# A transformer layer on one core: the same operations with a new issue order, new PSUM banks and eviction engines, and another pairing of the first layer's remainders

## The chip, the core and the metric

The kernel runs on one core of a Trainium2 chip. TensorE (PE, with its weight loads shown as PEld) multiplies; VectorE (DVE), ScalarE (ACT) and GpSimd (POOL) work on elements; the queue of SyncE (SP) issues every DMA. Each engine takes its instructions strictly in the order in which they were written, and engines wait for each other through semaphores. The metric is the device time of one execution in microseconds: 462.19 us before, the median of three runs (461.88 to 462.23).

## The reference

The input x has 2048 rows of 576 (bfloat16). It is computed:

```python
h  = x + A(layernorm(x))
h2 = h + gelu(layernorm(h) @ w1 + b1) @ w2 + b2       # w1: 576 x 4608
```

A is attention with 32 heads of 18 over four segments of 512 rows, with a memory carried from segment to segment:

```python
for s in range(4):
    p = softmax(qs @ ks.T * scale + causal_mask);  a_dot = p @ vs
    a_mem = (phi(qs) @ M) / (phi(qs) @ z + 1e-6)
    outs.append(g * a_mem + (1 - g) * a_dot)
    M += phi(ks).T @ vs;  z += phi(ks).sum(rows)
return concat(outs) @ wo                              # phi(t) = t+1 if t > 0 else exp(t)
```

## The kernel before

The rows are worked in eight chunks of 256, each of two tiles of 128 rows. For each tile: a layernorm (DVE statistics at L874/L883, POOL for the root at L878/L879, DVE or ACT to apply it at L887/L895), a transpose of the result (on PE at L910 for the first tiles, by a DMA transpose at L570 later), the products with wqkv (L867/L868, five matmuls for a contraction of 576: four of 128 and one remainder), evictions of q, k and v from PSUM (L994 to L1012), and transposes of q and k into QT and KT (PE at L1032 or DMA at L570). Attention goes in 80 visits: a score group of 16 matmuls into the four banks of `st` (L1115, tiled by 32 rows), one exp on ACT (L1132), masks on POOL (L1136), and groups of weighted values into the bank `ox` (L1155, tiled by 32 columns). One set of `st` banks serves all visits, so a score group waits until the exp of the visit before has read it. L1199 to L1209 finish a head group; L1169 to L1190 are the memory's part; L1309 transposes the attention's output, L867 multiplies it with wo, L1321 adds x, and a second layernorm follows.

The first layer of the MLP multiplies by w1 in half-groups (class `Half`, L1370) of two column blocks of 128, 256 rows wide. Its contraction of 576 is four times 128 and a remainder of 64. There are two forms. `whole` does the five matmuls one after the other over the full array (L867, L868). Or the remainders of two half-groups are issued together as a `rest` of four matmuls (L1390, `tail`), which use the upper and the lower 64 rows of the array side by side, and the 16 main matmuls follow (L1396, `main`). The set `WHOLE` names the rests (by their number) that are not issued in that way but as `whole`. Bias and eviction are at L1472 (DVE) or L1470 (ACT), gelu at L1488 (ACT), the second layer at L1588 with its eviction at L1594, and the output stores at L1598/L1600. Weights of w1 come group by group through SP (L1355, with two tails at L1358), w2 once (L1364, L1726).

A planner inside the kernel (from L65 on) builds a list `ops` of some 2,590 operations; but the order in which they are issued is not the planner's. It is written out as the list `ORDER` (L1737), which holds numbers of that list, and the last lines issue them in that order under a manual schedule. Number 81 is a filler, a matmul of zeros (L1652) that PE runs while it waits at the start; it stands 29 times in the list. Three more tables change the operations themselves: `PLACE` gives the PSUM bank (0 to 2) for the n-th time that a bank is taken, where it is not the planner's own; `FLIP` lists evictions that go to the other engine of DVE and ACT (or of ACT and POOL); `WHOLE` as above. Semaphores follow from the data and the banks, so a new order or a new bank gives new waits.

```python
        if o.made in FLIP:
            o.issue = issue
...
            return dict.__getitem__(self, ("bank", PLACE.get(k.n, k[1])) if isinstance(k, Tok) else k)
...
            h.rest = o.made not in WHOLE and o
...
        for n in ORDER:
            ops[n].issue()
```

Of the kernel before, what the change touches and what calls it, by code (L numbers as in the profile page):

```python
# [16 lines left out]
def kernel(  # L17
# [118 lines left out]
    class Tok(tuple):  # L136
# [22 lines left out]
    }  # L159
    FLIP = {  # L160
# [5 lines left out]
    }  # L166
    WHOLE = {
        2534, 2535, 2536, 2537, 2539, 2542, 2544, 2548, 2550, 2551, 2552, 2565, 2567, 2575,
# [1554 lines left out]
    for j, one in sorted(bulk.items()):  # L1723
# [182 lines left out]
```

## Time and profile before

| | before |
|---|---|
| reported time, median of 3 | 462.19 us |
| span of the profiled execution | 458.6 us |
| busy PE / ACT / DVE / POOL | 451.2 / 329.6 / 272.8 / 223.1 us |
| moved by DMA | 78.39 MB, mean 171 GB/s |
| granted TensorE clock | 1.000 over the span |

The span runs from the first to the last instruction; the reported time has some 3.6 us more around it. "Busy" is the time in which an engine has an instruction under way. A matmul's duration in the trace (0.27 us for 256 columns) is longer than its distance to the next one (0.11 us), since matmuls are pipelined: for the length of PE's work the starts count, not the durations. A row of the timeline is: start, time until the last of the group ends, engine, line, operation, what it writes and reads, shapes, count, and in brackets the idle time before it with what ended that. "SPq" is the queue in which DMAs are issued.

### The profile page before, as it was taken

How to read it: one execution, taken by the hardware profiler on the slowest of the kernel's cores; microseconds unless marked ns; L12 is line 12 of the kernel's file. 1: busy time of each engine (PE TensorE's matmuls, PEld its weight loads, DVE VectorE, ACT ScalarE, POOL GpSimd, SP SyncE). 2: the span in 40 equal slices, each digit the busy share in tenths (PEclk: the TensorE clock that was granted, in tenths of full speed). 3: DMA queues.
4: the chain of work that ended last, by engine and by line, in shares of the span. 5: the costliest groups of instructions: out<-in, count | busy, mean ns of one | idle time of the engine just before them, and what ended most of it. 6: DMA issues, size and time to landing. Idle time of an engine off the chain costs nothing.

```text
span 458.6 us, 14459 instructions
## 1 busy us (share of the span) xinstructions
PE 451.2 (98%) x6102; PEld 338.9 (74%) x6102; DVE 272.8 (59%) x604; ACT 329.6 (72%) x324; POOL 223.1 (49%) x378
## 2 busy tenths in 40 slices
PE   7998999999999999999999999999999999999997
PEld 5655688676787776777677767777777778888876
DVE  6897888887765686776566587655454323321111
ACT  8887888997698977979678897787756513363610
POOL 5785667687756478874545578764151100000000
PEclk9999999999999999999999999999999999999999
DMA  8689987958887934968778577965665439773011
GB/s 223 179 150 262 263 245 184 257 127 198 162 189 157 253 87 137 186 172 197 155 131 182 161 166 168 222 202 177 158 188 161 143 97 226 223 230 92 27 53 51
DMA packets 113091, 78.39 MB, mean 171 GB/s; under 512 B 47571, under 2 KB 110979, under 8 KB 113027
## 3 DMA queue, kind: packets, MB, share of 16 engines
q1 hardware_dynamic: 113027, 77.48, 68.6%
q8 instruction: 47, 0.77, 0.7%
q14 instruction: 17, 0.14, 0.1%
HBM read 60.09 MB, written 7.08 MB: 146 GB/s over the span
## 4 chain that ended last, share of the span: by engine, by line
PE 94%; DMA 2%; DVE 2%; ACT 1%; SPq 1%; issue 1%; ACTq 0%
PE bank L1588 23%; PE bank L867 20%; PE bank L1396 16%; PE last L1588 6%; PE st L1115 6%; PE bank L868 5%; PE ox L1155 5%; PE last L1396 4%; PE bank L1390 3%; PE ox L1588 2%; PE bank L1184 1%; DMA KT<-hT 1%; PE ox L1396 1%; DMA x_b<-in_A_x_dram 1%; ACT pt L1132 1%; PE bank L1080 1%
## 5 line engine op out<-in xcount | busy, mean ns | idle before, releaser
L1132 ACT ACTIVATE pt<-st 128x2048 bf16<-128x2048 f32 x80 | 150.1, 1877 | 41.0 <-PE st L1115 37.9
L1588 PEld LDWEIGHTS <-hT 128*128 128x128 bf16 x1188 | 112.0, 98 | 26.5
L1588 PE MATMUL bank<-w_sb,hT 128*128 128x288 bf16 (+1 forms) x864 | 121.8, 284 | 0.0
L1136 POOL TENSOR_SCALAR_AFFINE_SELECT pt<-pt 128x512 bf16<-128x512 bf16 x128 | 80.1, 640 | 51.5 <-ACT pt L1132 46.8
L1472 DVE TENSOR_TENSOR hT<-bank,b1T 128x512 bf16<-128x512 f32 x96 | 65.3, 687 | 60.7 <-PE bank L1396 48.9
L1396 PEld LDWEIGHTS <-w1g 128*128 128x128 bf16 x672 | 62.4, 98 | 15.1 <-issue 7.2
L1396 PE MATMUL bank<-xn2T,w1g 128*128 128x256 bf16 x576 | 72.7, 273 | 0.0
L1488 ACT ACTIVATE hT<-hT 128x1536 bf16<-128x1536 bf16 (+4 forms) x25 | 66.2, 2661 | 4.3 <-DVE hT L1472 4.1
L867 PE MATMUL bank<-wqkv,xT 128*128 128x432 bf16 (+2 forms) x256 | 56.0, 341 | 0.9 <-DVE xT L968 0.5
L867 PEld LDWEIGHTS <-xT 128*128 128x128 bf16 x392 | 35.9, 98 | 21.5 <-DVE xT L968 0.8
L1470 ACT ACTIVATE hT<-bank,b1T 128x256 bf16<-128x256 f32 x46 | 19.3, 472 | 33.4 <-PE bank L1396 24.8
L1115 PE MATMUL st<-QT,KT 32*128 32x128 bf16 x1280 | 32.3, 217 | 1.7 <-DMA KT<-hT 1.3
L867 PE MATMUL bank<-xn2T,w1g 128*128 128x256 bf16 (+1 forms) x264 | 33.8, 260 | 0.0
L1588 PE MATMUL last<-w_sb,hT 128*128 128x288 bf16 (+1 forms) x252 | 33.4, 277 | 0.0
L1174 POOL TENSOR_TENSOR pq<-ek,pq 128x512 bf16<-128x512 bf16 x24 | 28.0, 1167 | 7.5 <-DVE ek L1172 6.7
L1115 PEld LDWEIGHTS <-KT 32*128 32x128 bf16 x1280 | 18.7, 92 | 16.9 <-issue 11.1
L1199 DVE STREAM_TRANSPOSE ox<-ox 128x512 f32<-128x512 f32 x32 | 23.3, 728 | 11.4 <-PE ox L1155 11.4
L867 PEld LDWEIGHTS <-w1g 128*128 128x128 bf16 x272 | 24.0, 98 | 3.5
L1155 PE MATMUL ox<-pt,v_aug 128*19 128x128 bf16 x1280 | 25.8, 220 | 0.0
L1321 DVE TENSOR_TENSOR h_t<-bank,x_b 128x288 f32<-128x288 f32 x32 | 14.3, 454 | 18.8 <-PE bank L868 15.5
L1155 PEld LDWEIGHTS <-v_aug 128*19 128x19 bf16 x1280 | 17.9, 91 | 9.1 <-issue 7.4
L1209 POOL TENSOR_TENSOR o_nat<-t,t 128x288 bf16<-128x288 f32 x24 | 19.1, 794 | 9.4 <-DVE t L1208 9.3
(143 smaller groups left out, 666.5 us busy)
## 6 DMA issues: line engine op xcount, KB each, us to landing
w1g<-in_B_w_dram SPq DMA_DIRECT2D x57, 512.0 KB, 4.1
w_sb<-in_B_w_dram SPq DMA_DIRECT2D x12, 432.0 KB, 4.8
wqkv<-in_B_w_dram SPq DMA_DIRECT2D x10, 512.0 KB, 5.0
hd<-h_t SPq DMA_DIRECT2D x16, 288.0 KB, 3.2
hc<-hd SPq DMA_DIRECT2D x32, 144.0 KB, 2.4
w1g<-in_B_w_dram SPq DMA_DIRECT2D x114, 32.0 KB, 3.3
x_b<-in_A_x_dram SPq DMA_DIRECT2D x18, 144.0 KB, 3.6
hT<-in_B_w_dram SPq DMA_DIRECT2D x5, 512.0 KB, 5.1
```

The costliest lines, as they stand in the source:

```text
L867: nc.tensor.matmul(out=out_ap, lhsT=lhsT_of(slice(0, P), k), rhs=rhs_of(slice(0, P), k), start=(k == 0), stop=False)
L868: nc.tensor.matmul(out=out_ap, lhsT=lhsT_of(slice(0, rest), 4), rhs=rhs_of(slice(0, rest), 4), start=False, stop=True)
L1115: nc.tensor.matmul(out=st4[:, i, n * P:(n + 1) * P], lhsT=KTs[(2 * (c - c % 2) + kt) % NK][rows, g, :], rhs=QTs[(2 * c + qt) % NQ][rows, g ...
L1132: op("ACT", 1.88, lambda: nc.scalar.activation(out=pt[:], in_=st4[:], func=ACT.Exp, scale=scale), sk, [("pt", slot, n) for n in range(4)], ...
L1136: op("POOL", 0.65, lambda n=n: nc.gpsimd.affine_select(out=pt[:, :, n * P:(n + 1) * P], in_=pt[:, :, n * P:(n + 1) * P], pattern=[[0, 4], ...
L1155: nc.tensor.matmul(out=ox[32 * i:32 * i + E, (g % 4) * P:(g % 4) * P + P], lhsT=v_augs[(2 * s0 + kt) % NV][:, G * i + g, :], rhs=pts[slot] ...
L1174: op("POOL", 1.16, lambda: nc.gpsimd.tensor_tensor(out=pq[:], in0=e_g, in1=pq[:], op=ALU.add), ["ek"], ["pq"], slack=due("add"))
L1199: op("DVE", 0.73, lambda: nc.vector.transpose(out=ox[:], in_=ox[:]), [], ["ox"], slack=slack)
L1396: nc.tensor.matmul(out=self.acc[:, a, :], lhsT=self.wt[:, k, f:f + P], rhs=xn2T[self.c % 4][:, k, :], start=False, stop=(k == 3), skip_gro ...
L1472: either((0.684, lambda: nc.vector.tensor_tensor(out=dst, in0=acc(), in1=bias, op=ALU.add)), (nj * (0.22 + w * 0.00098), by_act), [b, "b1T ...
L1488: op("ACT", (f1e - f0) * Q * 0.00083 + 0.18, lambda: nc.scalar.activation(out=hT[:, f0:f1e, :], in_=hT[:, f0:f1e, :], func=ACT.Gelu_apprx_ ...
L1588: nc.tensor.matmul(out=bank_of(b)[:, 0:w], lhsT=hT[:, q, tl * P:(tl + 1) * P], rhs=w2_sb[:, q, hs], start=(q == 0), stop=(q == NF - 1))
```

## The change

The four tables are replaced; every other line stays (below the tables the line numbers rise by one). `ORDER` holds the same 2,558 numbers before and after, and 2,479 places hold another number. `PLACE` grows from 154 to 196 entries and `FLIP` goes from 79 to 75. `WHOLE` loses six of its numbers and gains one. Cut to the beginnings of the long tables:

```diff
     PLACE = {
-        6: 1, 7: 0, 10: 2, 11: 0, 12: 1, 15: 1, 16: 0, 19: 0, 20: 2, 22: 1, 23: 0, 26: 2, 31: 2, 32: 0, 39: 0, 40: 2,
...
+        3: 2, 5: 1, 7: 2, 8: 0, 11: 1, 12: 2, 15: 2, 16: 0, 17: 2, 19: 1, 21: 1, 22: 0, 23: 2, 24: 1, 25: 1, 27: 2,
...
     }
     FLIP = {
-        137, 161, 169, 189, 191, 221, 223, 234, 236, 238, 264, 266, 346, 422, 424, 426, 433, 436, 493, 642, 665, 667,
...
+        103, 137, 163, 177, 179, 189, 191, 221, 223, 234, 238, 264, 266, 348, 399, 422, 426, 436, 665, 671, 675, 678,
...
     }
     WHOLE = {
-        2534, 2535, 2536, 2537, 2539, 2542, 2544, 2548, 2550, 2551, 2552, 2565, 2567, 2575,
+        2534, 2536, 2539, 2542, 2548, 2550, 2552, 2565, 2570,
     }
...
     ORDER = [
-        1, 24, 26, 19, 0, 21, 22, 20, 81, 2, 81, 81, 46, 81, 64, 3, 81, 81, 62, 5, 81, 65, 18, 34, 81, 81, 8, 44, 81,
-        29, 81, 66, 4, 73, 51, 81, 11, 30, 81, 49, 9, 81, 31, 67, 81, 35, 59, 32, 81, 7, 81, 36, 54, 81, 23, 10, 81,
...
+        8, 19, 62, 24, 27, 23, 81, 81, 26, 11, 51, 81, 81, 81, 56, 52, 0, 49, 20, 42, 81, 25, 44, 81, 81, 48, 29, 28,
+        21, 22, 1, 2, 81, 81, 81, 81, 81, 81, 81, 55, 30, 81, 31, 5, 81, 18, 64, 81, 34, 3, 81, 81, 81, 81, 81, 81,
...
     ]
```

In the built kernels this gives, engine by engine:

- PE: 6,102 matmuls in both. L867/L868 lose 100, L1396/L1390 gain 80 and 20. Groups in a tiled mode go from 166 to 171 (42 to 47 of them remainders), entries into one from the full array from 97 to 93.
- SP: 392 entries in both. The first loads are x_b0, x_p0, x_p1 and then wq, where they were x_p1, x_p0 and then wq. The DMA transpose of the third K tile (KT2) stands 31st among the DMAs instead of 35th, right behind a 512 KB load of w1; one slice of wo now stands behind it.
- The first xT is copied from PSUM by ACT (L969) instead of DVE (L968); the transposes of the third tile stand ahead of the k products instead of behind them.
- Evictions of the first layer on DVE (L1472) go from 110 to 106, the ACTIVATEs of L1470 on ACT from 68 to 76; table loads of ACT are 22 in both.

291 rows, old and new, of tables (FLIP, ORDER, PLACE) are left out of this document.

## The prediction

> **What bounds the kernel now.** I read the page first (busy times), then the busy times by stretch, then who waited for whom on PE, then the timeline at the places that these name.
>
> ```profile
> span 458.6 us, 14459 instructions
> ...
> PE 451.2 (98%) x6102; PEld 338.9 (74%) x6102; DVE 272.8 (59%) x604; ACT 329.6 (72%) x324; POOL 223.1 (49%) x378
> ...
> L1132 ACT ACTIVATE pt<-st 128x2048 bf16<-128x2048 f32 x80 | 150.1, 1877 | 41.0 <-PE st L1115 37.9 <-PE ox L1155 1.2 <-POOL pt L1136 0.8
> ```
>
> ```profile
> 0.00:20.00 20.00, 17.47 (x160) 11.74 (x161) 13.67 (x41) 16.07 (x30) 12.39 (x31) 1.00 0.77 206
> 20.00:40.00 20.00, 18.31 (x298) 10.70 (x296) 17.05 (x43) 16.37 (x22) 14.69 (x29) 1.00 0.82 174
> 40.00:60.00 20.00, 19.67 (x379) 14.07 (x377) 16.79 (x42) 18.53 (x18) 13.72 (x25) 1.00 1.04 277
> 60.00:110.00 50.00, 49.98 (x814) 38.23 (x811) 41.98 (x93) 45.18 (x40) 36.20 (x59) 1.00 0.83 193
> ```
>
> The columns are the stretch, then the busy time of PE, PEld, DVE, ACT and POOL, the granted clock, the DMA share and GB/s. PE idles 7.4 us of the span. The first three stretches hold 2.53 + 1.69 + 0.33 = 4.55 us of it; the other 2.85 us is almost all the last eviction and store behind the last matmul. From 60 us on PE never runs dry, at full clock. So the time is the length of the PE stream plus a few waits in the first 60 us:
>
> ```profile
> PE st L1115 <- DMA KT<-hT: 1.3, 1, 1.3
> PE bank L867 <- DVE xT L968: 0.5, 1, 0.5
> PE bank L867 <- DVE hT L994: 0.3, 1, 0.3
> PE bank L910 <- DVE xn L887: 0.3, 1, 0.3
> PE st L1115 <- ACT pt L1132: 0.2, 1, 0.2
> ```
>
> A change of order can therefore gain in two ways only: a shorter stream, or fewer of these waits. It can lose by a new wait anywhere. Span and reported time differ by 462.19 - 458.6 = 3.6 us around the execution; I reckon all changes on the span and apply them to the median.
>
> **The change, part by part.** The same 2,558 issues stand in a new order; no data, tile or DMA is added. Four things move.
>
> *Length of the PE stream.* Matmuls follow each other at a fixed pitch, and each group in a tiled mode (scores by 32 rows, weighted values by 32 columns, first-layer remainders by 64 rows) costs a start and an end:
>
> ```profile
> 100.09 1.14 PE L1588 MATMUL bank<-w_sb,hT 128*128 128x288 bf16 x8
> 101.07 0.60 PE L867 MATMUL bank<-xn2T,w1g 128*128 128x256 bf16 x4
> 101.51 0.27 PE L868 MATMUL bank<-xn2T,w1g 128*128 128x256 bf16 x1
> 101.62 0.60 PE L867 MATMUL bank<-xn2T,w1g 128*128 128x256 bf16 x4
> ...
> 115.75 0.78 PE L1588 MATMUL bank<-w_sb,hT 128*128 128x288 bf16 x5
> 116.46 0.39 PE L1390 MATMUL bank<-xn2T,w1g 64*128 64x256 bf16 x4
> 116.79 0.61 PE L1396 MATMUL bank<-xn2T,w1g 128*128 128x256 bf16 x4
> ...
> 228.29 0.40 PE L1115 MATMUL st<-QT,KT 32*128 32x128 bf16 x16
> 228.63 0.39 PE L1390 MATMUL bank<-xn2T,w1g 64*128 64x256 bf16 x4
> 228.96 0.83 PE L1396 MATMUL bank<-xn2T,w1g 128*128 128x256 bf16 x6
> ```
>
> The first number is the start; start to start is what counts. Eight matmuls of 288 columns take 0.98 us, 0.1225 each; five of 256 take 0.55, 0.109 each. Four paired remainders take 0.325 us (116.46 to 116.79, 228.63 to 228.96). Entering a tiled mode from full mode costs another 116.46 - 115.75 - 5 x 0.1225 = 0.10 us; entering it from another tiled mode costs nothing more. The order of instructions of the two built kernels gives the counts. WHOLE shrinks from 14 to 9 entries, so 20 remainders that ran as full-array matmuls (L867/L868 fall by 100, L1396/L1390 rise by 80 and 20) run as five more groups of four. Minus 20 x 0.109 = -2.18, plus 5 x 0.325 = +1.63. Entries from full mode fall from 97 to 93: -0.4. Sum **-0.95 us**. Nothing hides this term and it needs no wait to go away.
>
> Here the Trainium skill speaks against it: TensorEngine Tiling (Array Packing), Tiling Modes, says that changing the mode drains the array, while its Overview promises up to 2x for a contraction of 64. By the 2x alone five groups would bring 5 x 0.218 = 1.09 us, an estimate; the trace agrees that a drain is paid, for the group takes 0.325 and not 0.218 us.
>
> *The head.* Loads, memsets and evictions of the first 10 us are reordered.
>
> ```profile
> 6.37 0.44 PE L910 MATMUL bank<-ident,xn 128*128 128x128 bf16 x5
> ...
> 7.58 0.69 ACT L969 COPY xT<-bank 128x640 bf16<-128x640 bf16 x1 [0.18 <-PE bank L910]
> 7.61 0.46 DVE L874 BATCH_NORM_STATS2 stats_p<-x_b 128x6 f32<-128x288 bf16 x1 [0.57 <-DMA x_b<-in_A_x_dram]
> ...
> 7.99 0.47 DVE L968 COPY xT<-bank 128x640 bf16<-128x640 bf16 x1
> ...
> 8.17 0.40 ACT L821 COPY w1g<-pq 64x256 bf16<-64x256 bf16 x1
> ...
> 8.48 0.56 ACT L821 COPY hT<-pq 128x448 bf16<-128x448 bf16 x1
> 8.52 0.91 PE L867 MATMUL bank<-wqkv,xT 128*128 128x432 bf16 x4 [0.53 <-DVE xT L968]
> ```
>
> ```profile
> 9.44 0.89 PE L867 MATMUL ox<-wqkv,xT 128*128 128x432 bf16 x4
> ...
> 10.58 0.89 PE L867 MATMUL bank<-wqkv,xT 128*128 128x432 bf16 x4
> ```
>
> Before, DVE sat on the load of x_b and copied the first xT only at 7.99, so the first real matmul came at 8.52. Afterwards ACT copies it: from some 7.1 (transposes at about 6.6, as DVE has two more memsets ahead) to 7.8. But ACT then has two L821 zeroings before the second xT: 7.8 + 0.40 + 0.56 + 0.69 = 9.45, when the second tile's matmul can start. That is 9.44 again. What is won is room: the transposes of a third tile (five, 0.28 us by the pitch of 128 columns, half of 256's) now stand ahead of the wk group instead of behind it, in place of two fillers of 0.22 us together. The wk group starts at about 10.64 instead of 10.58, with 0.28 us less behind it: **-0.2 us**. Bounds: +0.7 if the wq load, which now has a third 144 KB tile ahead of it, holds the first matmul (144 KB at 206 GB/s), and -0.7 if both xT come early (8.52 to 7.8).
>
> *The waits from 20 to 60 us.*
>
> ```profile
> 25.20 2.70 SPq L1358 DMA_DIRECT2D hT<-in_B_w_dram  x1
> ...
> 31.20 1.27 SPq L570 DMA_TRANSPOSE KT<-hT  x1
> ```
>
> ```profile
> 27.18 0.40 ACT L1005 CAST hT<-bank 128x288 bf16<-128x288 f32 x1 [0.26 <-PE bank L868]
> ...
> 27.49 0.89 PE L867 MATMUL bank<-wqkv,xT 128*128 128x432 bf16 x4 [0.35 <-DVE hT L994]
> ...
> 34.92 0.29 PE L1115 MATMUL st<-QT,KT 32*128 32x128 bf16 x8
> ...
> 36.55 0.29 PE L1115 MATMUL st<-QT,KT 32*128 32x128 bf16 x8 [1.34 <-DMA KT<-hT]
> ```
>
> The transpose of the third K tile has its data at 27.58 but is issued at 31.20 and lands at 36.55, 5.35 us later; PE has stood still since about 35. A score group takes 0.34 us (228.29 to 228.63), this one 1.85: 1.5 us lost. On SP it was the 35th DMA; now it is the 31st, and 528 KB less is queued ahead (one w_sb third, wo slices and w1 tails moved behind it). In the new order SP reaches it at 26 to 28 us and then waits for the data, so issue at 27.6 and landing near 33. Adding pitches from the wk group, its reader stands at 33.9. I take the 1.5 us as gone. Bounds: 0 (below) and -1.5.
>
> Against that, by the Trainium skill's DMA: Bandwidth & Descriptors (Queues, rings and completion order), each DMA engine takes one queue's descriptors in ring order, and a 512 KB w1 load now stands right before the transpose. By that rule alone it would land up to 2.9 us (512 KB at 174 GB/s, an estimate) later, and the stall would stay; but the 5.35 us of the row already has a large load ahead of it, so I keep the row.
>
> The 0.5 us at 27.49 (the bank's eviction queued on DVE behind gate work) has its evictions and banks changed, with 2.6 us of stream between; it may go (-0.5) or return elsewhere. What is late next is ACT: each score group waits for the exp before it (1.88 us), and ACT is 82% and 93% busy in these two stretches. With the K wait gone it has 1.5 us less room. The shortest stretch of stream between two score groups there is 2.35 us, a little under what one exp plus its handover needs, against two such places before. I charge 0.3 us for new waits on ACT and nothing for the 0.5 us: **-1.2 us** for this part, bounds +0.5 and -2.3.
>
> *Eviction engines and banks elsewhere.* Four net first-layer evictions move from DVE to ACT (two ACTIVATEs of 0.47 us for one DVE add of 0.69) and some casts move both ways: ACT gains about 1.7 us, DVE loses 2.5. I cost this at nothing: ACT idles 41.0 us before its exps, waiting for PE. Without that cover it would cost 1.7 us. Weight loads keep their distance:
>
> ```profile
> w1g<-in_B_w_dram SPq DMA_DIRECT2D x57, 512.0 KB, 4.1
> ...
> w1g<-in_B_w_dram SPq DMA_DIRECT2D x114, 32.0 KB, 3.3
> ```
>
> The shortest stream between the release ahead of a w1 load on SP and its reader is 5.6 us for 512 KB (5.3 before) and 4.2 for a tail (4.7 before): both over the time to land.
>
> **Sum.** -0.95 - 0.2 - 1.2 = -2.35 us: 462.2 - 2.35 = **459.8 us**.
>
> **Rivals.** *The stall is handed on* (20%): K lands early, but ACT at 93% cannot follow, or the 512 KB load delays K; only stream and head remain: 462.2 - 1.15 = 461.0. For it: the ACT column. Against it: ACT's work between the first and eleventh exp, counted from the two orders at the mean durations of its groups, falls by 0.5 us.
>
> *No waits at all* (15%): everything between 20 and 60 us goes too, 0.5 + 1.5 + 0.8 (the 0.33 idle after 40 us and the waits hidden under a matmul's latency): 462.2 - 1.15 - 2.8 = 458.2. Against it: ACT again.
>
> *Slower: the last wo slice* (10%). It is now issued behind the K transpose, at 28.9 at the earliest, and the first wo matmul stands at 32.8. With K's 5.35 us to land it comes at 34.3, 1.5 us late; if SP is also held as at 25.20 (2.70), 4.2 us late: 459.8 + 4.2 = 464.0. PE does nothing else in that time, since its order is fixed, and scores, exps and h queue behind. It makes the kernel slower once the slice is more than 2.4 us late. Against it: with 528 KB less ahead the ring should not be full there, and a plain load of 144 KB is lighter than a transpose.
>
> **How the numbers follow.** Forecast 55%, its own range 459.0 to 460.8. A measurement tells about 0.2% (0.9 us) from no change, so 461.3 is the edge. Forecast and no-waits are faster; of the handed-on case half. Faster 0.78, same 0.12, slower 0.10. The range 458.0 to 462.1 holds all but the slower case and little else.
>
> **What would show it.** The PE groups should read x912 on the first-layer main line and x228 on the remainders, with 0.325 us per four. The first wqkv matmul should start near 7.8 and the wk group near 10.6. The wait of st on KT should be gone, and the waits from 20 to 60 us should sum to under 1 us, now on ACT. From 60 us PE should stay at 100%. A wait on wo_t near 33 us, or any DMA wait beyond 60 us, would make the forecast wrong.

## The result, and the profile after

The changed kernel takes 458.17 us (median of 4 runs, 457.18 to 459.97) against 462.21 us before (4 runs, 461.88 to 462.34): a ratio of 0.992, 95% interval 0.9899 to 0.9941, so 4.0 us less (2.7 to 4.7). The forecast was 459.8 us, a ratio of 0.995, with a range of 458.0 to 462.1. A second measurement, of the unaltered pair beside the experiments, gave 458.99 us (6 runs, 458.01 to 460.74) against 461.52 us (23 runs, 460.41 to 463.58): 0.9947, interval 0.9927 to 0.9968, 2.5 us less (1.5 to 3.4). Both intervals hold a gain of about 3 us, a little more than the 2.35 us that I had summed.

The page of the changed kernel, its span, the busy times and ACT's largest group:

```profile
span 455.3 us, 14477 instructions
...
PE 450.7 (99%) x6102; PEld 337.4 (74%) x6102; DVE 271.3 (60%) x602; ACT 330.3 (73%) x327; POOL 223.7 (49%) x381
...
L1133 ACT ACTIVATE pt<-st 128x2048 bf16<-128x2048 f32 x80 | 150.1, 1876 | 36.2 <-PE st L1116 30.3
```

The span is 3.3 us shorter (458.6 to 455.3). PE is still the bound; its idle time falls from 7.4 to 4.6 us. ACT idles 36.2 us before its exps instead of 41.0 (30.3 of it put down to the scores on PE, 37.9 before), so it kept most of its slack. By stretches (the columns as in the prediction: stretch, busy time of PE, PEld, DVE, ACT, POOL, clock, DMA share, GB/s):

```profile
0.00:20.00 20.00, 18.42 (x162) 11.74 (x163) 14.50 (x43) 16.54 (x31) 12.62 (x34) 1.00 0.81 207
20.00:40.00 20.00, 20.00 (x334) 12.24 (x333) 18.37 (x45) 18.05 (x24) 16.64 (x30) 1.00 0.89 200
40.00:60.00 20.00, 19.96 (x420) 14.73 (x419) 17.72 (x40) 18.30 (x18) 12.56 (x23) 1.00 0.98 232
60.00:110.00 50.00, 50.00 (x781) 37.42 (x782) 42.15 (x95) 42.96 (x35) 35.62 (x57) 1.00 0.88 217
110.00:200.00 90.00, 89.90 (x1292) 65.41 (x1288) 60.99 (x142) 77.28 (x74) 61.83 (x101) 1.00 0.72 162
```

PE's idle time from 20 to 40 us went from 1.69 us to nothing, from 40 to 60 us from 0.33 to 0.04. In 0 to 20 us it fell by 0.95, half of it because PE's fillers start 0.5 us earlier, which moves no later work. Who waited for whom, with microseconds, times and the longest:

```profile
PE st L1653 <- DVE pq L802: 1.2, 1, 1.2
...
PEld L1391 <- DMA w1g<-in_B_w_dram: 0.4, 2, 0.3
...
PE ox L868 <- ACT xT L970: 0.3, 1, 0.3
```

The first row is the wait for the fillers' zeros at the very start. The K wait (1.3 before) and the bank waits on DVE are gone. What is new is small and stands where I had said that nothing would: two first-layer remainders wait for w1 tails near 194 us. The places of the old stalls, in the timeline:

```profile
24.46 0.90 PE L868 MATMUL bank<-wqkv,xT 128*128 128x432 bf16 x4
...
25.39 0.89 PE L868 MATMUL bank<-wqkv,xT 128*128 128x432 bf16 x4
...
26.31 0.89 PE L868 MATMUL bank<-wqkv,xT 128*128 128x432 bf16 x4
```

```profile
26.81 1.25 SPq L571 DMA_TRANSPOSE KT<-hT  x1
...
28.11 0.58 SPq L756 DMA_DIRECT2D wo_t<-in_A_wo_dram  x1
...
32.78 0.65 PE L868 MATMUL bank<-wo_t,xT 128*128 128x288 bf16 x4
...
33.94 0.40 PE L1116 MATMUL st<-QT,KT 32*128 32x128 bf16 x16
```

The groups that stalled at 27.49 before now run at their pitch (24.46, 25.39, 26.31: 0.92 for five matmuls of 432 columns). K is issued at 26.81 instead of 31.20, and its scores (33.94) run in one piece. The wo slice behind it at 28.11, my slower rival, was in time here. The first wqkv groups of the two tiles and the wk group behind them:

```profile
7.88 0.89 PE L868 MATMUL bank<-wqkv,xT 128*128 128x432 bf16 x4
...
9.28 0.91 PE L868 MATMUL ox<-wqkv,xT 128*128 128x432 bf16 x4 [0.30 <-ACT xT L970]
...
10.48 0.65 PE L868 MATMUL bank<-wqkv,xT 128*128 128x288 bf16 x4
```

The 3.3 us of the two profiled executions fall apart as follows. The two stalls that are gone were 1.5 and 0.5 us; the small waits that are left after the head sum to about 0.9 us in both (each start-to-start time less its pitch, added up over all matmuls): -2.0. The wk group starts at 10.48 instead of 10.58 with five transposes (0.28) already behind it: -0.4. The last eviction and store take the same time. The remaining -0.9 is the shorter stream. Counted directly, with the usual pitch of each kind of matmul and group, the 6,102 matmuls add up to 447.0 us before and 446.0 after, 1.0 less. Its pitches are as forecast, here a group next to another tiled group and one entered from full mode:

```profile
129.10 0.39 PE L1391 MATMUL bank<-xn2T,w1g 64*128 64x256 bf16 x4
129.42 1.92 PE L1397 MATMUL bank<-xn2T,w1g 128*128 128x256 bf16 x16
131.18 2.12 PE L1589 MATMUL bank<-w_sb,hT 128*128 128x288 bf16 x16
133.24 0.39 PE L1391 MATMUL bank<-xn2T,w1g 64*128 64x256 bf16 x4
```

Four remainders take 0.32 us (129.10 to 129.42), and entering costs 133.24 - 131.18 - 16 x 0.1225 = 0.10.

### The profile page after: what moved, and what is told of

Read it like the earlier page. It is cut to its first block, busy times and chain, and to the rows that moved or that the text cites. A ratio compares the mean times of both kernels' runs of the same rounds, so it can differ in the third digit from the quotient of the medians.

```text
span 455.3 us, 14477 instructions
## 1 busy us (share of the span) xinstructions
PE 450.7 (99%) x6102; PEld 337.4 (74%) x6102; DVE 271.3 (60%) x602; ACT 330.3 (73%) x327; POOL 223.7 (49%) x381
## 4 chain that ended last, share of the span: by engine, by line
PE 97%; DMA 1%; ACT 0%; SPq 0%; DVE 0%; issue 0%
PE bank L1589 23%; PE bank L868 19%; PE bank L1397 18%; PE last L1589 6%; PE st L1116 6%; PE ox L1156 5%; PE bank L869 5%; PE last L1397 4%; PE bank L1391 3%; PE ox L1589 2%; PE bank L1185 1%; PE st L1653 1%; DMA w1g<-in_B_w_dram 1%; PE ox L1397 1%; PE bank L1033 1%; PE bank L1081 1%
## 5 line engine op out<-in xcount | busy, mean ns | idle before, releaser
L1133 ACT ACTIVATE pt<-st 128x2048 bf16<-128x2048 f32 x80 | 150.1, 1876 | 36.2 <-PE st L1116 30.3
L1473 DVE TENSOR_TENSOR hT<-bank,b1T 128x512 bf16<-128x512 f32 x93 | 63.5, 688 | 67.2 <-PE bank L1397 58.2
L1397 PE MATMUL bank<-xn2T,w1g 128*128 128x256 bf16 x640 | 80.7, 273 | 0.0
L1397 PEld LDWEIGHTS <-w1g 128*128 128x128 bf16 x736 | 68.7, 98 | 15.3 <-issue 6.3
L868 PE MATMUL bank<-wqkv,xT 128*128 128x432 bf16 (+2 forms) x256 | 56.0, 341 | 0.0
L868 PEld LDWEIGHTS <-xT 128*128 128x128 bf16 x392 | 35.9, 98 | 20.8 <-ACT xT L970 0.8
L1471 ACT ACTIVATE hT<-last,b1T 128x256 bf16<-128x256 f32 x18 | 7.4, 474 | 38.2 <-PE last L1397 38.2
L1589 PE MATMUL last<-w_sb,hT 128*128 128x288 bf16 (+1 forms) x252 | 34.9, 278 | 0.0
L1471 ACT ACTIVATE hT<-bank,b1T 128x256 bf16<-128x256 f32 x52 | 21.7, 472 | 14.0 <-PE bank L1397 13.1
L1116 PEld LDWEIGHTS <-KT 32*128 32x128 bf16 x1280 | 18.6, 92 | 15.3 <-issue 10.7
L1595 DVE TENSOR_TENSOR ot<-bank,hc 128x288 bf16<-128x288 f32 (+1 forms) x24 | 10.7, 444 | 27.4 <-PE bank L1589 24.1
L868 PE MATMUL bank<-xn2T,w1g 128*128 128x256 bf16 (+1 forms) x200 | 24.9, 255 | 0.0
L1339 POOL TENSOR_TENSOR h_t<-h_t,b_bc 128x576 f32<-128x576 f32 x16 | 20.5, 1281 | 8.5 <-DVE xn L888 8.2
```

The lines of the kernel that those rows point to most:

```text
L868: nc.tensor.matmul(out=out_ap, lhsT=lhsT_of(slice(0, P), k), rhs=rhs_of(slice(0, P), k), start=(k == 0), stop=False)
L1116: nc.tensor.matmul(out=st4[:, i, n * P:(n + 1) * P], lhsT=KTs[(2 * (c - c % 2) + kt) % NK][rows, g, :], rhs=QTs[(2 * c + qt) % NQ][rows, g ...
L1133: op("ACT", 1.88, lambda: nc.scalar.activation(out=pt[:], in_=st4[:], func=ACT.Exp, scale=scale), sk, [("pt", slot, n) for n in range(4)], ...
L1397: nc.tensor.matmul(out=self.acc[:, a, :], lhsT=self.wt[:, k, f:f + P], rhs=xn2T[self.c % 4][:, k, :], start=False, stop=(k == 3), skip_gro ...
L1471: nc.scalar.activation(out=dst[:, j, :], in_=acc()[:, j, :], func=ACT.Identity, bias=b1T[:, j0 + j:j0 + j + 1], scale=1.0)
L1473: either((0.684, lambda: nc.vector.tensor_tensor(out=dst, in0=acc(), in1=bias, op=ALU.add)), (nj * (0.22 + w * 0.00098), by_act), [b, "b1T ...
```

## The experiments

Each time stands beside that of the kernel before, measured with it; rows with the same time of before were measured together.

| version | us (runs) | before, us | ratio, 95% |
|---|---|---|---|
| changed kernel again | 458.99 (6) | 461.52 | 0.9947 [0.9927, 0.9968] |
| before, K earlier, wo tail behind it | 462.05 (12) | 461.52 | 1.0008 [0.9995, 1.002] |
| before, the new WHOLE | 468.83 (5) | 461.52 | 1.0155 [1.0132, 1.0178] |
| changed, eight more pairs | 461.39 (12) | 461.52 | 1.0016 [0.999, 1.0043] |
| before, K and wo tail earlier | 460.71 (12) | 461.39 | 0.9982 [0.9972, 0.9993] |
| the same, one cast earlier | 461.03 (12) | 461.39 | 0.999 [0.9979, 1.0] |
| before, xT copy ahead of x_b | 461.07 (12) | 461.39 | 0.9993 [0.9981, 1.0006] |
| changed, zeroings behind xT | 459.02 (11) | 461.39 | 0.9953 [0.9934, 0.9971] |
| before again | 461.74 (1) | | |
| before, w1 tails first | 461.64 (12) | 461.82 | 0.9986 [0.997, 1.0002] |
| changed, two DMAs moved | 457.96 (6) | 461.82 | 0.9911 [0.9887, 0.9935] |
| the same, w1 tails first | 457.18 (6) | 461.82 | 0.9892 [0.9869, 0.9915] |

### The two kernels, profiled again

Neither is edited.

> The changed kernel, unaltered. Theory (the time is the length of PE's stream plus a few waits, and what varies between executions is waits on loads): 458.2 us median again, executions between 457 and 460; a longer span than 455.3 shows as more or longer PE waits behind loads beyond 60 us, w1g above all, while the first 60 us and the pitch of the stream stay as they were. Rival (the head varies, by when the first loads land): the difference stands ahead of the wk group at 10.5 us. Rival (the four times were a chance draw): a median at 459.5 or more.

> The kernel before, unaltered, for a second look at its waits. Theory (the profile from which the forecast was made is an execution at the fast end; loads of w1 come late in the usual one): a span of 459.2 us or more, a PE wait on w1g of 0.3 us or more near 244 or 332 us, and the first wqkv matmul after 8.6 us. Rival (those waits belong to the variants only): waits as in the first profile, 0.2 us at 244 and none at 332.

The kernel before, second profile, its span and PE's waits on DMA:

```profile
span 459.6 us, 14459 instructions
...
PE bank L868 <- DMA wo_t<-in_A_wo_dram: 1.3, 1, 1.3
...
PE bank L1390 <- DMA w1g<-in_B_w_dram: 0.6, 1, 0.6
```

And at the places themselves:

```profile
35.79 0.30 PE L868 MATMUL bank<-wo_t,xT 128*128 128x288 bf16 x1 [1.33 <-DMA wo_t<-in_A_wo_dram]
...
243.81 0.28 PE L1390 MATMUL bank<-xn2T,w1g 64*128 64x256 bf16 x1
244.69 0.39 PE L1390 MATMUL bank<-xn2T,w1g 64*128 64x256 bf16 x3 [0.60 <-DMA w1g<-in_B_w_dram]
245.01 1.16 PE L1396 MATMUL bank<-xn2T,w1g 128*128 128x256 bf16 x9
```

Two things follow. First, the 1.5 us stall is not K's alone: in this execution it is the last tail of wo (18 KB) that holds PE, and K, which lands next, costs nothing more. Both are issued behind the same 432 KB w2 third, and either can come last: in the five profiles that keep this part of the order PE stands on K twice and on the wo tail three times, for 1.1 to 1.5 us. Second, the execution from which I forecast was at the fast end: this one loses 0.9 us near 244 us (245.01 - 243.81 = 1.20 for a group that takes 0.325), the first 0.2. Its time is 461.74 us, 2.1 above its span, so of the 3.6 us between my profile's span and the median only some 2 lie around the execution; the other 1.5 are time inside the usual execution that this profile did not have. The first wqkv matmul, at 8.57, was not later than in the first profile: that part of the expectation failed here.

The changed kernel, second profile (span 456.8 us, 1.5 more than the first):

```profile
PE st L1116 <- DMA KT<-hT: 0.4, 1, 0.4
```

```profile
33.05 0.41 PE L868 MATMUL bank<-wo_t,xT 128*128 128x288 bf16 x2
33.69 0.41 PE L868 MATMUL bank<-wo_t,xT 128*128 128x288 bf16 x2 [0.23 <-DMA wo_t<-in_A_wo_dram]
```

So my slower rival does occur, in small: two matmuls of 0.1225 and then 0.4 us of standing until 33.69. The fourth K tile costs 0.6 us at 52 us (0.1 in the first profile), the head 0.3. Another 0.8 us stands at 70 and 77 us, with no load named for it; what it is stays open. So part of what varies are loads, as the theory has it, but not those of w1, and these lie ahead of 60 us; the 0.8 us beyond it is not shown to be a load.

### The K transpose alone, earlier

SP's order, before to this version:

```diff
 x_b (144 KB)
+KT transpose (third tile)
 w1 tail
 w2 third (432 KB)
 wo slice
 wo tail (18 KB)
 w1 tail, w1 tail
-KT transpose (third tile)
```

> The kernel before, with the transpose of the third K tile issued five DMAs earlier on SP (ahead of two w1 tails, one w2 third, the last wo slice and a third w1 tail) and nothing else. Theory (its lateness costs 1.5 us and nothing else is near): the wait of st on KT goes, 462.2 - 1.5 = 460.7 us, the 0.5 us at 27.5 stays. Rival (the stall is handed on): new PE waits on ACT of 1 us or more within the next 10 us, 461.7 to 462.2 us. Rival (the loads ahead of it, not its issue, set when it lands): KT is issued near 27.6 and lands at 35 or later, 461.5 us or more.

Nothing was gained (462.05 against 461.52). K is issued at 28.43 and no longer waited for, but the wo tail stands behind it:

```profile
36.81 0.28 PE L868 MATMUL bank<-wo_t,xT 128*128 128x288 bf16 x1 [1.46 <-DMA wo_t<-in_A_wo_dram]
```

All three theories missed: the stall went neither away nor to ACT, and K was not late (its semaphore has the full count at 31.67). It went to the next load in the queue, 1.6 us start to start. The changed order had moved the wo tail as well, from 32nd to 24th on SP, which I had not counted.

### K and the wo tail earlier

```diff
 x_b (144 KB)
 w1 tail
-w2 third (432 KB)
 wo slice
 wo tail (18 KB)
-w1 tail, w1 tail
 KT transpose (third tile)
+w2 third (432 KB)
+w1 tail, w1 tail
```

> The kernel before with the transpose of the third K tile three DMAs earlier on SP, as in the last attempt, but with the tail of wo (18 KB) left ahead of it: only a w2 third (432 KB) and two w1 tails (64 KB) stand behind it now. Theory (the last attempt lost because the tail of wo, moved behind K, came late in its stead): no DMA wait of PE between 28 and 40 us, 1.1 to 1.5 us less than before, so 460.2 us where before reads 461.5. Rival (whatever comes last on the DMA queues at 33 to 37 us holds PE): a wait on wo_t or on KT of 1 us or more stays, 461.5 us. Rival (handed on to ACT): waits of st on pt of 1 us or more between 37 and 50 us.

```profile
34.73 0.29 PE L868 MATMUL bank<-wo_t,xT 128*128 128x288 bf16 x1
...
35.40 0.40 PE L1115 MATMUL st<-QT,KT 32*128 32x128 bf16 x16
```

The DMA waits between 28 and 40 us are gone whole, as the theory wants, and none came on ACT. But the time moved by 0.7 us (0.3 to 1.3), less than the 1.1 to 1.5 expected, though the interval reaches into that range. In this version's profile:

```profile
PE bank L1390 <- DMA w1g<-in_B_w_dram: 0.8, 2, 0.4
...
PE bank L867 <- DMA w1g<-in_B_w_dram: 0.3, 1, 0.3
```

Start to start, PE loses 2.0 us on w1 loads at 135, 244 and 332 us, against 0.9 in the second profile of before. Part of the gain may have been handed to w1 loads later on, where the order is unchanged. That is not shown: the version with K alone gained nothing and loses 0.9 us on w1 at 332 as well, so these loads may only have come late in these executions. The changed kernel has its own order in those stretches.

### The cast that holds a bank at 27.5 us

On top of the last version, on DVE:

```diff
 L1199 StreamTranspose ox
+L994 TensorCopy hT<-bank 128x432
 L851 TensorScalarPtr omg
 L1200 Reciprocal r
-L994 TensorCopy hT<-bank 128x432
 L1206 TensorTensor o_nat
```

> The same, and the eviction of the third Q/K group's second half (DVE cast of 128x432) issued ahead of the last gate piece and the reciprocal on DVE instead of behind them. Theory (that cast, late on DVE, holds the bank for which PE waits 0.5 us at 27.5): the wait there shrinks by 0.35 to 0.4 us, 0.4 us less than the version above. Rival (PE's order decides, by which two groups on the same bank stand too near each other): the wait shrinks by under 0.1 us and the time is that of the version above.

The wait at 27.5 shrank as expected, from 0.49 to 0.18 us, and the time did not fall (461.03 against 460.71):

```profile
28.70 0.40 PE L1155 MATMUL ox<-pt,v_aug 128*19 128x128 bf16 x16 [0.20 <-DVE o_nat L1206]
...
31.36 0.89 PE L867 MATMUL bank<-wqkv,xT 128*128 128x432 bf16 x4 [0.50 <-DVE MZacc L1087]
```

What comes behind the cast on DVE is late next: 0.3 us at 28.70, 0.7 at 31.36. The changed kernel got rid of the wait another way: PE takes three Q/K/V groups in a row on three banks (24.46 to 26.31 above) and the cast has a group's time more. That this is the cause is read from the two orders; PE's order alone wasn't tried.

### Pairing alone

```diff
     WHOLE = {
-        2534, 2535, 2536, 2537, 2539, 2542, 2544, 2548, 2550, 2551, 2552, 2565, 2567, 2575,
+        2534, 2536, 2539, 2542, 2548, 2550, 2552, 2565, 2570,
     }
```

> The kernel before with the changed kernel's WHOLE, 9 entries, and nothing else: 20 remainders run in five more tiled groups, here without fewer entries from full mode (97 as before). Theory (pitch alone): 20 x 0.109 less, 5 x 0.325 more, -0.55 us: 461.65 us, no new waits. Rival (a pair opens two banks at once, so PE waits for an eviction at the new groups): new waits at the remainders' line of 0.5 us or more in all, 462.2 us or over.

It costs 7 us. Timeline of PE and the busy times by stretch:

```profile
136.99 0.61 PE L1390 MATMUL bank<-xn2T,w1g 64*128 64x256 bf16 x4 [3.37 <-DMA w1g<-in_B_w_dram]
...
138.61 3.60 PE L1396 MATMUL bank<-xn2T,w1g 128*128 128x256 bf16 x16
142.00 1.86 PE L1588 MATMUL bank<-w_sb,hT 128*128 128x288 bf16 x12
```

```profile
133.00:137.00 4.00, 0.63 (x42) 0.46 (x34) 0.61 (x3) 3.98 (x2) 1.92 (x3) 0.83 0.99 212
137.00:142.00 5.00, 5.00 (x40) 3.01 (x41) 1.42 (x2) 3.10 (x3) 0.00 (x0) 0.50 0.02 6
142.00:150.00 8.00, 8.00 (x94) 6.19 (x92) 6.46 (x16) 2.74 (x2) 3.60 (x9) 0.97 0.78 184
```

Neither theory had this. A pair's remainders are issued at the place where their number stands in ORDER, ahead of both main parts; while the number is in WHOLE the place does nothing, so in the old order it stands anywhere. Here it stands where the w1 load has not landed: 3.4 us of waiting. Then the clock is at half for 5 us (its reading is in the last section). So WHOLE can't be changed without ORDER, and this run is no price of pairing. The price stays the one read from the pitches.

### Eight more pairs in the changed kernel

```diff
     WHOLE = {
-        2534, 2536, 2539, 2542, 2548, 2550, 2552, 2565, 2570,
+        2548,
     }
```

This version leaves out parts of the first layer's sums. By my reading, which no run shows, the remainders of the added pairs are written into PSUM banks that other groups still use at that place. The instructions and their number stand.

> The changed kernel with only one entry left in WHOLE: 32 more remainders run in tiled groups, 96 entries from full mode against 93. Theory (pitch alone): 32 x 0.109 = 3.49 less; eight more groups of four, two of which only lengthen a group that stands, so 8 x 0.218 + 6 x 0.107 more, and 3 x 0.10 for the entries: -0.81 us, 457.4 us against the changed kernel's 458.2. Rival (these eight stand where both banks are not free in time): waits of PE at the remainders' line that eat it, 458.2 us or more.

```profile
PE bank L1391 <- DMA w1g<-in_B_w_dram: 1.3, 2, 0.8
...
PE bank L1391 <- DMA hT<-in_B_w_dram: 0.7, 1, 0.7
...
PE bank L1391 <- DMA xn2T<-xn: 0.5, 1, 0.5
```

The rival holds, by data more than by banks: 461.39 us, and the same cause as above. The pitches offer a reason why nine pairs are left whole: four remainders cost 4 x 0.109 = 0.436 us in full mode and 0.325 + 0.10 = 0.425 in a group of their own. Only beside another tiled group is there much to gain.

### The head

In the kernel before, on DVE:

```diff
 L887 TensorScalarPtr xn
-L874 BNStats x_b
 L968 TensorCopy xT<-bank
+L874 BNStats x_b
```

> The kernel before with one DVE instruction moved: the first statistics of x_b behind the first xT copy instead of ahead of it. Theory (in the order before, the load of x_b holds DVE and with it the first real matmul, by an amount that differs between executions: 8.52, 9.05 and 9.45 us in three profiles): the first wqkv matmul at 7.6 to 7.9 us, the second at 8.5 to 8.9, the wk group at 9.7 to 10.1, so 0.9 us or more less than before: 460.5 us where before reads 461.5. Rival (the loads of wq and wk set the head): the wk group stays at 10.5 or later, 461.3 us or more.

In the changed kernel, on ACT:

```diff
 L970 TensorCopy xT (first tile)
-L822 TensorCopy hT<-pq 64x256
-L822 TensorCopy hT<-pq (pads)
 L970 TensorCopy xT (second tile)
+L822 TensorCopy hT<-pq 64x256
+L822 TensorCopy hT<-pq (pads)
```

> The changed kernel with two ACT zeroings (0.40 and 0.56 us) moved from ahead of the second xT copy to behind it. Theory (they alone hold the second tile's matmul): the copy at 7.8 to 8.0 us instead of 8.5 to 8.8, its matmul straight behind the first tile's, the wk group at 10.0 instead of 10.5: 0.5 us less than the changed kernel, 458.5 us where before reads 461.5. Rival (the wk load or the third tile's normalization comes last): the wk group stays at 10.4 or later, 459.0 us.

The kernel before with the copy moved, its first and its wk group:

```profile
7.76 0.89 PE L867 MATMUL bank<-wqkv,xT 128*128 128x432 bf16 x4
...
8.68 0.90 PE L867 MATMUL ox<-wqkv,xT 128*128 128x432 bf16 x4
...
10.17 0.89 PE L867 MATMUL bank<-wqkv,xT 128*128 128x432 bf16 x4 [0.19 <-DMA wqkv<-in_A_wk_dram]
```

The changed kernel with the zeroings moved:

```profile
10.75 0.65 PE L868 MATMUL bank<-wqkv,xT 128*128 128x288 bf16 x4 [0.18 <-DMA wqkv<-in_A_wk_dram]
```

In the kernel before the first matmuls came as early as the theory says (7.76; the second straight behind at 8.68); in the changed one the second came straight behind the first, but that only at 8.29. Then both wait for the wk load: it lands at about 10.2 and 10.7. For the changed kernel that is the rival. For the kernel before neither text has it: the wk group, at 10.17, missed the 9.7 to 10.1 of the theory and came 0.8 us ahead of its mean in seven profiles (10.97), yet the time hardly fell; where the 0.8 us went isn't shown. Neither time differs from that of its unaltered kernel (461.07 against 461.39, with an interval that holds 1.0; 0.9953 against 0.9947). So the wk load limits what an earlier xT can win. The unaltered changed kernel did not wait for it in its two profiles (10.48 and 10.75, straight behind the third tile's transposes).

### The w1 tails, and two DMAs of the changed kernel

For 89 tails of the kernel before, and in the last version for 66 of the changed one:

```diff
+w1 tail (32 KB), w1 tail (32 KB)
 w1 tile (512 KB)
-w1 tail (32 KB), w1 tail (32 KB)
```

> The kernel before with 89 of its w1 tails (32 KB) issued ahead of the 512 KB load of their w1 tile instead of behind it, from the second round of the buffers on. Theory (the waits at 244 and 332 us are of remainders, which come first in their pair, for tails that queue behind the 512 KB): both waits fall under 0.2 us, 0.5 to 1.2 us less than before: 460.6 us where before reads 461.4. Rival (the 512 KB loads, now later, come late in their stead): waits at the main line's L1396 or L867 as long as those at L1390 were; 461.4 us or more.

```profile
135.32 0.78 PE L1588 MATMUL bank<-w_sb,hT 128*128 128x288 bf16 x5
137.03 0.61 PE L867 MATMUL bank<-xn2T,w1g 128*128 128x256 bf16 x4 [0.93 <-DVE stats_p L874]
```

The waits at the remainders fell to 0.2 us at 245 and none at 332, as the theory wants, but a whole (unpaired) first-layer group now stands still for 1.1 us at 137. The timeline names a DVE instruction; the view of waits names, for the weight loads of this line, the load of w1, and that is the rival's mark:

```profile
PEld L867 <- DMA w1g<-in_B_w_dram: 1.2, 1, 1.2
```

The time is 461.64 against 461.82 us: undecided, and far from what was hoped.

For the changed kernel, on SP:

```diff
 wo slice
+wo slice (the one from behind KT)
 x_b
 w1 tile (512 KB)
 KT transpose (third tile)
-wo slice
...
 KT transpose (fifth tile)
-w2 third (432 KB)
 KT transpose (fourth tile)
+w2 third (432 KB)
```

> The changed kernel with two DMAs moved on SP: the wo slice that stood behind the third K transpose now stands ahead of the 512 KB w1 load, and one w2 third (432 KB) stands behind the fourth K transpose instead of ahead of it. Theory (in its usual execution the changed kernel waits for these two at 33.7 to 34.4 us, 0.4 to 1.1 us, and at 51 to 52 us, 0.1 to 0.6 us): no wait on wo_t, under 0.2 us on KT at 52, 0.5 us less than the changed kernel: 458.4 us where before reads 461.4. Rival (K or another load comes late instead, or the waits return further on): 459.0 us.

> The same, and 66 w1 tails issued ahead of their 512 KB load. Theory (what is left of the changed kernel's waits beyond 60 us, 0.4 to 0.9 us in its profiles, is remainders waiting for tails): another 0.3 us less, 458.1 us, and executions closer together. Rival (the 512 KB loads come late in their stead): the same as the version above or slower, with waits at the main line.

The first of the two takes 457.96 us, ratio 0.9911; the second 457.18, ratio 0.9892. In the first one's profile PE waits for no load of 0.3 us or more, neither wo_t nor KT; its stretch from 20 to 40 us:

```profile
20.00:40.00 20.00, 20.00 (x330) 12.05 (x329) 18.30 (x45) 18.17 (x23) 16.61 (x30) 1.00 0.86 197
```

In the second one's, PE is fully busy in every stretch from 60 to 410 us, but waits for xT transposes at 20 and 47 us:

```profile
PE bank L868 <- DMA xT<-xn: 1.1, 2, 0.6
```

Both beat the kernel before; against the changed kernel the second one's interval ends (0.9915) below where that of the second measurement begins (0.9927) but overlaps that of the first (0.9899 to 0.9941). The two are not told apart from each other, and that the executions came closer together is not shown: six each lie within 1.8 and 2.3 us (457.26 to 459.03, 456.29 to 458.55), six of the changed kernel within 2.7.

## Why the prediction was right, point by point

*What bounds the kernel.* Right: PE's stream and a few waits in the first 60 us. One sentence was too strong: "From 60 us on PE never runs dry" held for the profiled execution only. Even there the view of waits has 0.2 us for w1 at 244. The second profile of before loses 0.9 us near 244 us, and the changed kernel's own profile 0.4 near 194, which by my last sentence would have made the forecast wrong. It was too small to do so.

*Span and median.* "462.19 - 458.6 = 3.6 us around the execution" is a step that failed. Around the execution lie some 2 us (461.74 and 459.6; 457.18 and 455.3). The other 1.5 us belong to the usual execution, with waits such as that of 0.9 us near 244. The changed kernel's profile is of a fast execution too, the fastest of its four (457.18), but only 1.0 us under the median. Such waits are part of why the medians of the first measurement moved by more than the spans; the second measurement moved by less, so how much is not settled.

*The stream, -0.95.* Right: 208 remainders in groups became 228 and 832 main matmuls 912, with the pitches as forecast; 0.9 us are left for it when the waits and the head are taken off, and the pitches of all matmuls add up to 1.0 less. One wording was loose: "entering it from another tiled mode costs nothing more" holds because the 0.325 us of a group already have its leaving in them, about 0.10 us, which falls away only when the next group is in the same mode. No run isolates the term: the run with WHOLE alone paid for misplaced remainders.

*The head, -0.2.* Right in mechanism, undersized: -0.4 between the two profiles, because the second tile's matmul came at 9.28 instead of the 9.45 that I had. Over seven profiles with the old head the first matmul starts at 8.52 to 9.45, 8.91 in the mean, and the wk group 2.06 us behind it; over five of the changed head the wk group starts at 10.48 to 11.03, 10.73 in the mean, with the 0.28 us of transposes done. That is -0.5 in the mean. My profile was the best of the seven, since x_b's load came early in it. The forecast "-0.7 if both xT come early" was tried and meets the wk load.

*The waits from 20 to 60 us, -1.2.* The step that was mis-sized; it measured -2.0 in the first profiles (PE's idle time there went from 1.69 + 0.33 to 0.04 us). Between the second profiles of the two kernels it is -1.3 (1.66 + 0.33 to 0.23 + 0.45), close to the forecast, so the -2.0 is partly the luck of a good execution. The K stall was 1.5 us as forecast and is gone. "I charge 0.3 us for new waits on ACT and nothing for the 0.5 us" was wrong in both parts: no wait longer than 0.13 us was added there in the first profile, those of the second (0.4 us on the wo slice, 0.6 on the fourth K tile) are on loads and not on ACT, and the 0.5 us went entirely. Why K's move works I had only half: K and the wo tail are both late behind the w2 third, and only the order that takes both forward removes the stall (K alone: no gain; both: no DMA wait there).

*The ring.* By the Trainium skill's DMA: Bandwidth & Descriptors (Queues, rings and completion order), each DMA engine takes the descriptors of one queue in ring order. From that I had estimated that the 512 KB load ahead of K would put its landing off by up to 2.9 us, to more than 8 us after its issue. The estimate failed: K was issued at 26.81 and read at 33.94, 7.1 us later, with no wait, and in none of the six profiles of the changed kernel and its variants did PE wait for it at that place. The rule itself is not contradicted. The 512 KB load had been issued at 24.17, 2.6 us ahead of K, and landed at 29.72; by its semaphore K landed at 30.6, right behind it. I had charged K with the load's whole 2.9 us, though the load had been under way for 2.6 us when K was issued.

*The rivals.* "No waits at all" came nearest in the first measurement: 458.2 for it, 458.17 measured. I gave it 15% because of ACT, and ACT was no obstacle. That the numbers meet so closely is in part luck: the second measurement, with 2.5 us less, lies nearest to the forecast's 2.35, and the two profiles lie between them, 3.3 us apart. "The last wo slice" is real, at 0.4 us in the second profile and 0.9 us of waiting in the version with the zeroings moved, but short of the 2.4 us from which it would have decided. "Handed on" did not happen in the changed kernel; it happened in several of my own edits.

## What to carry to other kernels

Before forecasting from one profile, look where its time lies among the timed runs: at the fast end it lacks waits that the usual execution has, and they sit where a load lands only just in time. Where several loads queue behind one large transfer, moving one of them forward uncovers the next; move all that are read in the same stretch, or the large one. An order that was tuned as a whole does not come apart: here the pairing table and the remainders' places could not be changed one without the other, and a cast moved forward on a busy engine only handed its lateness on.

## What the runs showed of the hardware that I had not expected

A wait of PE can cost more than its length. In the version with WHOLE alone PE stood still for 3.4 us, and for the 5 us from 137 on the granted clock was 0.50: sixteen matmuls of 256 columns took 142.00 - 138.61 = 3.39 us, 0.212 each instead of 0.109. By the pitches this added some 2.4 us to the 3.4. The waits of up to 1.6 us in the other versions left the clock at 1.00. The Trainium skill, TensorE: Matmul & The Clock Gate (Part 1: The HAM clock gate), has this as a gate to half rate after at least one idle window of about 3.4 us. The trace agrees in the half rate, and less well in the length: a mean of 0.83 from 133 to 137 us, with 1.00 before the fall and 0.50 after it, puts the fall at about 135.6, when PE had stood still for 2.0 us (since 133.63).

Executions of one program, measured together, differ by 2 to 4 us at a granted clock of 1.00 (460.41 to 463.33 for the kernel before, 457.44 to 461.21 for the changed one with the zeroings moved). The slowest three of the kernel before (463.58, 464.71 and 464.88) have a mean clock of 0.995 or 0.996, so the clock fell for a short time in them too; none of the three was profiled. In the profiles it is the loads that land at other times in the same order: the stall near 35 us is on K in one execution and on the wo tail in the next, the same w1 load costs 0.2 or 0.9 us. Whether that is all of the spread isn't shown.
